# Remainder evictions of a six-layer cross network in pieces of 256 columns instead of 512

## The chip, the cores and the metric

The kernel runs on one core of a Trainium2 chip. The metric is the device time of one execution in microseconds (us), the median of several runs. A core has five engines that run their own queues of instructions and wait for one another by semaphores: TensorE (PE in the profile; its weight loads are PEld), VectorE (DVE), ScalarE (ACT), GpSimd (POOL) and SyncE (SP), which here issues most of the DMA transfers. Matrix products are summed in PSUM and leave it by an *eviction*: an instruction of ScalarE or VectorE that reads PSUM and writes SBUF.

## The reference

Six cross layers on 4096 rows of 416 columns, all in bf16:

```
B, F, D, L = 4096, 26, 16, 6        # Din = F * D = 416
x = x0
for l in range(6):
    x = x0 * (x @ ws[l] + bs[l]) + x
return x
```

ws[l] is 416 x 416, bs[l] has 416 entries.

## The kernel before

The kernel carries a sum c instead of x: with c the running sum of all (x @ ws + bs) plus one, the next x is x0 * c. The first five layers work on the transposed input, with features on the 128 partitions and rows of the batch along the free dimension; the last layer turns the product round, so that its results come out with batch rows on the partitions and can be stored.

416 features are three blocks of 128 (index m or k, NK = 3) and a remainder of 32. The batch of 4096 rows is two halves (s = 0, 1) of 2048, each of four groups (g) of 512 rows (CW). The main blocks of c and x are the tiles CM and XH. The remainder's 32 features would use a quarter of the partitions, so the four groups of a half are laid on partitions 32 g to 32 g + 31: the remainder of one half is a tile of 128 partitions by 512 columns, and both halves together are CR (c), XR (x).

In PSUM there is one pool of four buffers, each of two banks of 512 fp32 columns, which are given out in turn. A main tile (s, m) takes two buffers (h = 0, 1), the remainder sums of both halves take one (pr in layer 0, pr2 after it, one bank for each half).

Layer 0 (`first_layer`) works on XM0 as it arrives by DMA. In its second half (s = 1) the remainder sums of both halves are computed behind the main ones (`mm_rem`, lines 220 and 224) and evicted by `ew_rem`. Layers 1 to 4 take the six main tiles in pairs. TensorE multiplies the first tile's 48 matmuls (L208), then the rows that bring in the remainder of x for both tiles (L214, eight matmuls), then the second tile's 48. Behind the first pair of each layer stands `rem_pair`: the remainder sums of both halves, and their `ew_rem`.

A main eviction (`ew_main`, L187) is one ScalarE instruction over 1024 columns that adds the bias and writes a temporary tile t (a pool of six buffers); VectorE adds t to c (L188) and multiplies by x0 (L189), which gives the next x. `ew_rem` does the same for one half of the remainder with 512 columns: ScalarE L194 (layer 0, straight into CR) or L197 (into t), VectorE L198 (the addition, in layers 1 to 4) and L201 (the product with x0: in layer 0 two instructions of 256 columns, otherwise one of 512).

In layer 4 the finished c is sent back to batch rows by transposing DMAs from SP's queue: CM into XLrows, and CR into the scratch tiles scrR, whose rows ScalarE copies into XLrows by `xl_rem(s)` (L310). `xl_rem(0)` stands between two main evictions of layer 4, `xl_rem(1)` behind the last. The last layer (L359 to L380) sums into the tiles py; ScalarE casts them to bf16 (L405), VectorE adds XLrows (L407) and multiplies by the input rows (L395), and the result is stored (L396), the last piece by a DMA that ScalarE issues itself.

The order on each engine is the program's order where `pin` is used (`keep_in_program_order`); otherwise the tile framework may move an instruction.

Of the kernel before, what the change touches and what calls it, by code (L numbers as in the profile page):

```python
# [9 lines left out]
ACT = mybir.ActivationFunctionType  # L10
ALU = mybir.AluOpType
BF16 = mybir.dt.bfloat16
# [4 lines left out]
def kernel(  # L17
# [7 lines left out]
    nc = tc.nc  # L25
    B, D = x0.shape
    L = ws.shape[0]
    P = 128
    NK = 3
# [3 lines left out]
    NG = 4  # L33
    CW = 512
# [6 lines left out]
    tpool = ctx.enter_context(tc.tile_pool(name="tpool", bufs=6))  # L41
# [15 lines left out]
    bR = const.tile([P, L], FP32)  # L57
    X0rows = big.tile([P, NBT, D], BF16)
    XLrows = big.tile([P, NBT, D], BF16)
    scrR = [big.tile([P, 4, P], BF16, name=f"scrR{s}") for s in range(NS)]  # L60
# [5 lines left out]
    XR = [big.tile([P, NS * CW], BF16, name=f"XR{i}") for i in range(3)]  # L66
    CM = big.tile([P, NK, B], BF16, name="CM")
    CR = big.tile([P, NS * CW], BF16, name="CR")
# [11 lines left out]
    def pin(ins):  # L80
        tc.keep_in_program_order(ins)
# [33 lines left out]
    for g in range(1, NG):  # L115
        dst, src = WR[32 * g:32 * g + 32, 0, :], WR[0:R, 0, :]
# [73 lines left out]

    def ew_rem(l, s, pr, nxtR):
        cols = slice(CW * s, CW * s + CW)
        if l == 0:
            nc.scalar.activation(CR[:, cols], pr, ACT.Identity, bias=bR[:, 0:1], scale=1.0)  # L194
        else:
            tr = tpool.tile([P, 2 * CW], BF16, name="t")
            nc.scalar.activation(tr[:, 0:CW], pr, ACT.Identity, bias=bR[:, l:l + 1], scale=1.0)  # L197
            nc.vector.tensor_tensor(out=CR[:, cols], in0=tr[:, 0:CW], in1=CR[:, cols], op=ALU.add)  # L198
        for a in range(CW * s, CW * s + CW, CW if l else CW // 2):
            part = slice(a, a + (CW if l else CW // 2))  # L200
            prod = nc.vector.tensor_tensor(out=nxtR[:, part], in0=CR[:, part], in1=XR[0][:, part], op=ALU.mult)  # L201
            if l == 0:
                pin(prod)

    def mm_full(l, s, m, g, pts, cur, first, last):
        for k in range(NK):
# [27 lines left out]
    def first_layer(s):  # L234
# [53 lines left out]
        for m in range(2):  # L288
            ew_main(0, s, m, 1, pb[m], nxt)
        ew_rem(0, 0, pr[:, 0, :], nxtR)  # L290
        ew_main(0, s, 2, 1, pb[2], nxt)
        ew_rem(0, 1, pr[:, 1, :], nxtR)

    bias_setup()
# [4 lines left out]
    def rem_pair(l, cur, curR, nxtR, feeds_last):  # L299
        pr2 = psum.tile([P, 2, CW], FP32, tag="ps", name="pr2")  # L300
        for s in range(NS):
            mm_rem(l, s, pr2[:, s, :], cur, curR)
        for s in range(NS):
            ew_rem(l, s, pr2[:, s, :], nxtR)
            if feeds_last:
                nc.sync.dma_start_transpose(out=scrR[s][:], in_=CR[:, CW * s:CW * s + CW])

    def xl_rem(s):
        tc.keep_in_program_order(
            nc.scalar.copy(XLrows[:, 16 * s:16 * s + 16, NK * P:D].rearrange("p (g i) r -> p i g r", g=NG),  # L310
                           scrR[s][:].rearrange("p i (g r) -> p i g r", g=NG)))

    cur, curR = XH[0:2], XR[1]
    for l in range(1, LL):
        nxt, nxtR = [[h for h in XH if h is not cur[0] and h is not cur[1]][0], cur[0]], XR[1 + (l % 2)]
# [11 lines left out]
        for n in range(0, len(tiles), 2):  # L327
            ta, tb = tiles[n], tiles[n + 1]
            pts[ta] = new_pts()
            for g in range(NG):  # L330
                mm_full(l, ta[0], ta[1], g, pts[ta], cur, True, False)
            mm_row(l, ta[0], ta[1], pts[ta], curR, False, True)
            pts[tb] = new_pts()
            mm_row(l, tb[0], tb[1], pts[tb], curR, True, False)
            if feeds_last and n == 4:
                xl_rem(0)
            finish(ta)
            for g in range(NG):
                mm_full(l, tb[0], tb[1], g, pts[tb], cur, False, True)
            finish(tb)  # L340
            if n == 0:
                rem_pair(l, cur, curR, nxtR, feeds_last)
        if feeds_last:
            xl_rem(1)
        cur, curR = nxt, nxtR

    l = LL
# [123 lines left out]
```

## Time and profile before

| | |
|---|---|
| median of 3 runs (lowest, highest) | 130.42 us (130.15, 130.46) |
| the profiled execution | 130.23 us |
| its span, first to last instruction | 128.1 us |
| TensorE, VectorE, ScalarE, GpSimd busy | 123.5, 100.9, 86.2, 4.8 us |
| mean granted TensorE clock | 0.998 of full speed |
| ScalarE, 128 x 512 from PSUM, layers 1 to 4 (L197) | 8 times, 683 ns mean |
| ScalarE, 128 x 512 from PSUM, layer 0 (L194) | 2 times, 692 ns mean |
| ScalarE, copy 128 x 512 (L310) | 2 times, 626 ns mean |

A row of an engine's busy time counts each instruction from its start to its end; instructions that follow one another on ScalarE or VectorE overlap a little in the record. A row of instructions reads: line, engine, operation, output tile, input tiles, partitions and columns, how often, busy us, mean ns of one, and the idle time of the engine just before them with what ended it. A row of a timeline has the start in us, the length in us, the same names, and in brackets the idle time before it and its releaser.

### The profile page before, as it was taken

To read this page: it belongs to the slowest core of one execution; us is meant where nothing else is said; L and a number is where in the kernel's file an instruction comes from. 1 tells how busy PE (TensorE), PEld (TensorE's weight loads), DVE (VectorE), ACT (ScalarE), POOL (GpSimd) and SP (SyncE) were. 2 spreads that over 40 slices of the span, in tenths; PEclk is the share of its full clock that TensorE was granted. 3 is DMA by queue.
4 is the path that set the end of the run, shared out by engine and by line. 5 is a ranking of instruction groups with operands and counts; after the bars stand their busy time and mean duration, and the time that the engine had idled before them with its cause. 6 is when DMAs were issued, how large, how long until landed. Compare 5 with 4: busy or idle time off the path is not lost.

```text
span 128.1 us, 4002 instructions
## 1 busy us (share of the span) xinstructions
PE 123.5 (96%) x1708; PEld 55.9 (44%) x1710; DVE 100.9 (79%) x195; ACT 86.2 (67%) x98; POOL 4.8 (4%) x18
## 2 busy tenths in 40 slices
PE   7999999999999999999999999999999999999980
PEld 3343343444434444434444434444434445445450
DVE  0123579964979898989898989898989899988991
ACT  0048857878848668848668848668849696569660
POOL 4004001300000000000000000000000000000000
PEclk9999999999999999999999999999999999999999
DMA  3999999999940000000000000000498899976764
GB/s 93 234 234 224 174 238 259 318 332 336 336 144 0 5 0 0 8 0 5 0 5 0 5 0 5 0 0 5 86 125 192 161 135 236 199 231 220 228 194 142
DMA packets 42229, 16.37 MB, mean 128 GB/s; under 512 B 31034, under 2 KB 42212, under 8 KB 42212
## 3 DMA queue, kind: packets, MB, share of 16 engines
q1 hardware_dynamic: 37432, 15.40, 53.3%
q10 hardware_dynamic: 4780, 0.72, 3.6%
q8 instruction: 13, 0.21, 0.7%
q14 instruction: 4, 0.03, 0.1%
HBM read 6.15 MB, written 3.41 MB: 75 GB/s over the span
## 4 chain that ended last, share of the span: by engine, by line
PE 92%; DMA 4%; DVEq 1%; ACT 0%; issue 0%; DVE 0%
PE pt L208 50%; PE ph L240 13%; PE py L365 12%; PE pt L214 5%; PE pr L224 5%; DMA XM<-in_x_dram 4%; PE pr L220 2%; PE py L377 1%; PE ph L247 1%; PE py L380 1%; PE py L359 1%; DVEq L466 1%; PE tpr L163 1%; ACT t L405 0%; PE py L369 0%
## 5 line engine op out<-in xcount | busy, mean ns | idle before, releaser
L208 PE MATMUL pt<-XH,WM 128*32 128x512 bf16 x1152 | 65.2, 379 | 0.0
L187 ACT ACTIVATE t<-pt,bM 128x1024 bf16<-128x1024 f32 x48 | 49.6, 1115 | 19.3 <-PE pt L214 19.3
L208 PEld LDWEIGHTS <-WM 128*32 128x32 bf16 x1152 | 29.7, 97 | 33.8 <-issue 5.1
L188 DVE TENSOR_TENSOR CM<-t,CM 128x1024 bf16<-128x1024 bf16 x48 | 32.9, 686 | 5.1 <-ACT t L187 5.1
L189 DVE TENSOR_TENSOR XH<-CM,XM 128x1024 bf16<-128x1024 bf16 x48 | 33.2, 692 | 3.6
L405 ACT CAST t<-py 128x416 bf16<-128x416 f32 (+1 forms) x22 | 14.3, 649 | 5.1 <-PE py L365 2.0
L365 PE MATMUL py<-WM,XH 128*128 128x416 bf16 x90 | 17.0, 339 | 0.0
L240 PE MATMUL ph<-XM,WM 128*128 128x512 bf16 x70 | 16.3, 379 | 0.2
L181 ACT ACTIVATE CM<-ph,bM 128x1024 bf16<-128x1024 f32 x12 | 12.5, 1113 | 3.5 <-PE ph L247 3.5
L183 DVE TENSOR_TENSOR XH<-CM,XM 128x512 bf16<-128x512 bf16 x24 | 9.1, 438 | 3.6 <-ACT CM L181 3.6
L365 PEld LDWEIGHTS <-XH 128*128 128x128 bf16 x90 | 8.5, 98 | 7.6 <-issue 1.4
L240 PEld LDWEIGHTS <-WM 128*128 128x128 bf16 x72 | 6.8, 97 | 8.6 <-issue 1.1
L407 DVE TENSOR_TENSOR t<-t,XLrows 128x416 bf16<-128x416 bf16 (+1 forms) x20 | 9.3, 467 | 1.1 <-ACT t L405 1.1
L395 DVE TENSOR_TENSOR o<-t,X0rows 128x416 bf16<-128x416 bf16 (+1 forms) x22 | 9.9, 456 | 0.1
L214 PE MATMUL pt<-XR,WR 32*128 32x512 bf16 x96 | 7.3, 379 | 0.0
L224 PE MATMUL pr<-XH,WM 128*32 128x512 bf16 x96 | 6.6, 379 | 0.0
L197 ACT ACTIVATE t<-pr,bR 128x512 bf16<-128x512 f32 x8 | 5.1, 683 | 2.1 <-PE pr L224 2.1
L114 ACT ACT_TABLE_LOAD x1 | 1.3, 1283 | 6.1 <-DMA XM<-in_x_dram 6.1
L201 DVE TENSOR_TENSOR XR<-CR,XR 128x512 bf16<-128x512 bf16 (+1 forms) x12 | 4.4, 379 | 1.1 <-ACT CR L194 0.8
L224 PEld LDWEIGHTS <-WM 128*32 128x32 bf16 x120 | 3.2, 97 | 3.2
L148 PE MATMUL wps<-const-float32-1.0 128*128 128x512 f32 x4 | 3.8, 1094 | 0.8 <-PEq L455 0.8
L157 DVE CAST bM<-pb 128x18 f32<-128x18 bf16 x1 | 0.2, 177 | 4.9 <-PE pb L156 4.9
(52 smaller groups left out, 47.2 us busy)
## 6 DMA issues: line engine op xcount, KB each, us to landing
X0rows<-in_x_dram SPq DMA_DIRECT2D x8, 312.0 KB, 6.7
out_dram<-o SPq DMA_DIRECT2D x9, 208.0 KB, 3.2
WM<-in_ws_dram SPq DMA_DIRECT2D x5, 312.0 KB
out_dram<-o SPq DMA_DIRECT2D x13, 104.0 KB, 1.7
X0rows<-in_x_dram SPq DMA_DIRECT2D x4, 208.0 KB, 6.1
WR<-in_ws_dram SPq DMA_DIRECT2D x4, 130.0 KB, 4.8
WM<-in_ws_dram ACTq DMA_DIRECT2D x1, 312.0 KB
XM<-in_x_dram SPq DMA_TRANSPOSE x8, 5.7
```

Of the source, the lines that this page charges most:

```text
L181: nc.scalar.activation(c, src, ACT.Identity, bias=bias, scale=1.0)
L187: nc.scalar.activation(t[:], src, ACT.Identity, bias=bias, scale=1.0)
L188: nc.vector.tensor_tensor(out=c, in0=t[:], in1=c, op=ALU.add)
L189: nc.vector.tensor_tensor(out=x, in0=c, in1=XM0[:, m, c0:c0 + 2 * CW], op=ALU.mult)
L208: nc.tensor.matmul(pts[g // 2][32 * q:32 * q + 32, g % 2, :], lhsT=WM[:, l, k, 128 * m + 32 * q:128 * m + 32 * q + 32], rhs=cur[s][:, k, C ...
L214: nc.tensor.matmul(pts[g // 2][:, g % 2, :], lhsT=WR[32 * g:32 * g + 32, l, 128 * m:128 * m + 128], rhs=curR[32 * g:32 * g + 32, CW * s:CW ...
L224: nc.tensor.matmul(pr[32 * g:32 * g + 32, :], lhsT=WM[:, l, k, NK * P:D], rhs=cur[s][:, k, CW * g:CW * g + CW], start=False, stop=(k == NK ...
L240: nc.tensor.matmul(pt[:, gl, :], lhsT=WM[:, 0, k, 128 * m:128 * m + 128], rhs=cur[:, k, c0:c0 + CW], start=(k == 0 and not after_row), sto ...
L365: nc.tensor.matmul(py[:, 0:D], lhsT=q_x(q, g, k), rhs=WM[:, l, k, :], start=((not closes) and k == 0), stop=(closes and not adds and k == ...
L395: pin(nc.vector.tensor_tensor(out=o[:, 0:n, :], in0=src, in1=X0rows[:, b, :], op=ALU.mult))
L405: nc.scalar.copy(tv, src)
L407: pin(nc.vector.tensor_tensor(out=tv, in0=tv, in1=XLrows[:, rows(q, g0, n), :], op=ALU.add))
```

## The change

`ew_rem` evicts in two pieces of 256 columns. In layer 0 each of the two products of 256 columns can begin when its piece is there; in layers 1 to 4 the addition and the product stay whole. `xl_rem(0)` copies in two pieces (two of the four row blocks each), `xl_rem(1)` in one as before. ScalarE has 11 more instructions: two in layer 0, eight in layers 1 to 4, one for the copy.

```
     def ew_rem(l, s, pr, nxtR):
         cols = slice(CW * s, CW * s + CW)
+        halves = [slice(a, a + CW // 2) for a in range(0, CW, CW // 2)]
+        base = CR[:, cols] if l == 0 else tpool.tile([P, 2 * CW], BF16, name="t")
+        for a in halves:
+            nc.scalar.activation(base[:, a], pr[:, a], ACT.Identity, bias=bR[:, l:l + 1], scale=1.0)
         if l == 0:
-            nc.scalar.activation(CR[:, cols], pr, ACT.Identity, bias=bR[:, 0:1], scale=1.0)
-        else:
-            tr = tpool.tile([P, 2 * CW], BF16, name="t")
-            nc.scalar.activation(tr[:, 0:CW], pr, ACT.Identity, bias=bR[:, l:l + 1], scale=1.0)
-            nc.vector.tensor_tensor(out=CR[:, cols], in0=tr[:, 0:CW], in1=CR[:, cols], op=ALU.add)
-        for a in range(CW * s, CW * s + CW, CW if l else CW // 2):
-            part = slice(a, a + (CW if l else CW // 2))
-            prod = nc.vector.tensor_tensor(out=nxtR[:, part], in0=CR[:, part], in1=XR[0][:, part], op=ALU.mult)
-            if l == 0:
-                pin(prod)
+            for a in halves:
+                part = slice(CW * s + a.start, CW * s + a.stop)
+                pin(nc.vector.tensor_tensor(out=nxtR[:, part], in0=CR[:, part], in1=XR[0][:, part], op=ALU.mult))
+            return
+        nc.vector.tensor_tensor(out=CR[:, cols], in0=base[:, 0:CW], in1=CR[:, cols], op=ALU.add)
+        nc.vector.tensor_tensor(out=nxtR[:, cols], in0=CR[:, cols], in1=XR[0][:, cols], op=ALU.mult)
...
     def xl_rem(s):
-        tc.keep_in_program_order(
-            nc.scalar.copy(XLrows[:, 16 * s:16 * s + 16, NK * P:D].rearrange("p (g i) r -> p i g r", g=NG),
-                           scrR[s][:].rearrange("p i (g r) -> p i g r", g=NG)))
+        dst = XLrows[:, 16 * s:16 * s + 16, NK * P:D].rearrange("p (g i) r -> p i g r", g=NG)
+        src = scrR[s][:].rearrange("p i (g r) -> p i g r", g=NG)
+        n = 4 if s else 2
+        for i in range(0, 4, n):
+            pin(nc.scalar.copy(dst[:, i:i + n], src[:, i:i + n]))
```

## The prediction

> **What bounds the kernel now.** I read the page's busy rows and its chain first, then the list of what TensorE waits for, then the code-load queues, and last the timelines of ScalarE, VectorE and TensorE around each remainder eviction. The page:
>
> ```profile
> span 128.1 us, 4002 instructions
> PE 123.5 (96%) x1708; PEld 55.9 (44%) x1710; DVE 100.9 (79%) x195; ACT 86.2 (67%) x98; POOL 4.8 (4%) x18
> ...
> q8 instruction: 13, 0.21, 0.7%
> q14 instruction: 4, 0.03, 0.1%
> ...
> PE 92%; DMA 4%; DVEq 1%; ACT 0%; issue 0%; DVE 0%
> ...
> L187 ACT ACTIVATE t<-pt,bM 128x1024 bf16<-128x1024 f32 x48 | 49.6, 1115 | 19.3 <-PE pt L214 19.3
> ...
> L197 ACT ACTIVATE t<-pr,bR 128x512 bf16<-128x512 f32 x8 | 5.1, 683 | 2.1 <-PE pr L224 2.1
> ```
>
> TensorE is busy 96% of the span and makes 92% of the chain that ended last; ScalarE is 0% of it, is busy 67%, and sits idle 19.3 us before the main evictions, each time released by TensorE (L214). The rows of TensorE's own waits are short:
>
> ```profile
> engine line waited for: us in total, times, longest us
> PE wps L148 <- PEq L455: 0.8, 1, 0.8
> ```
>
> Its only wait is the one before its first instruction. So nothing that ScalarE or VectorE does today holds TensorE up, and the question is whether the change makes it do so. ScalarE's timeline (start, length, then in brackets the idle time before), for the remainder pair of layer 0, the pair of layer 1, and the copy of remainder rows:
>
> ```profile
> 26.66 1.27 ACT L194 ACTIVATE CR<-pr,bR 128x512 bf16<-128x512 f32 x2
> 29.41 4.13 ACT L187 ACTIVATE t<-pt,bM 128x1024 bf16<-128x1024 f32 x4 [1.48 <-PE pt L214]
> 34.07 1.27 ACT L197 ACTIVATE t<-pr,bR 128x512 bf16<-128x512 f32 x2 [0.54 <-PE pr L224]
> 36.97 4.13 ACT L187 ACTIVATE t<-pt,bM 128x1024 bf16<-128x1024 f32 x4 [1.64 <-PE pt L214]
> ...
> 98.81 0.62 ACT L310 COPY XLrows<-scrR 128x512 bf16<-128x512 bf16 x1
> 100.52 4.13 ACT L187 ACTIVATE t<-pt,bM 128x1024 bf16<-128x1024 f32 x4 [1.09 <-PE pt L214]
> ```
>
> Behind each lies idle time that TensorE ends: 1.48, 1.64 and 1.09 us. The pairs of layers 2 to 4 (53.31, 72.55, 91.78) have 1.63 or 1.64 us behind them in the same timeline. The consumers in layer 1, on VectorE:
>
> ```profile
> 35.88 0.42 DVE L198 TENSOR_TENSOR CR<-t,CR 128x512 bf16<-128x512 bf16 x1
> 36.33 0.42 DVE L201 TENSOR_TENSOR XR<-CR,XR 128x512 bf16<-128x512 bf16 x1
> 36.67 0.42 DVE L198 TENSOR_TENSOR CR<-t,CR 128x512 bf16<-128x512 bf16 x1
> ```
>
> Neither add waits for ScalarE (no bracket): VectorE comes late to them from its own queue. And on TensorE, the rows that write the bank next:
>
> ```profile
> 28.98 0.61 PE L214 MATMUL pt<-XR,WR 32*128 32x512 bf16 x8
> ...
> 36.54 0.61 PE L214 MATMUL pt<-XR,WR 32*128 32x512 bf16 x8
> ```
>
> **The change, part by part: the evictions.** Ten evictions of 512 columns (two in layer 0, eight in layers 1 to 4) become twenty of 256. No row before has a 256-column ScalarE eviction, so I work it out. Four 1024-column evictions back to back take 4.13 us and one lasts 1.115, so they start (4.13 - 1.115) / 3 = 1.005 us apart. Two of 512 take 1.27 and one lasts 0.683, so they start 0.59 apart. That is 0.415 us for 512 columns, 0.81 ns a column, and some 0.17 us that each instruction costs whatever its size. A half then starts 0.59 - 0.21 = 0.38 after the one before and lasts 0.683 - 0.21 = 0.47. Four halves: 3 x 0.38 + 0.47 = 1.61 us in place of 1.27, so +0.34 a pair. Bounds: nothing (no cost beside the columns), and a half that costs as much as a whole, 3 x 0.59 + 0.68 = 2.45, so +1.18. I take +0.34, from the straight line through two rows of the same operation; over five pairs it is 1.7 us of ScalarE time.
>
> The Trainium skill's page "ScalarE: Activation LUTs" (Rules for kernel authors) has about 0.3 us for each ACTIVATE and 0.83 ns an element, and "VectorE: DVE Perf Modes" (The TRN2 errata) advises tiles of 512 elements or more since a fixed cost is paid per instruction: both speak against halves. The rows bear out the slope and have 0.17 of fixed cost between starts, against 0.3; by the page's figure a pair would cost +0.6, an estimate, inside the bounds above, and the time would be the same.
>
> What hides it, place by place. (1) ScalarE's queue: behind the pair stands the L187 eviction of the next main tile, which TensorE releases at 36.97. The halves end at 34.07 + 1.61 = 35.68, at worst at 36.52. (2) The bank: PSUM's four buffers go round in order, so the remainder pair's buffer is the one that the second half of the second following tile takes, four allocations on. The last two of the eight L214 matmuls write it first: 36.54 + 6 x 0.067 (0.54 / 8 from the chain) = 36.94. Released at 35.68, it leaves 1.26 us; at worst 0.42. (3) VectorE: its add for the first 512 columns begins at 35.88 and needs two halves, ready at 34.07 + 0.38 + 0.47 = 34.92 (worst 35.34); the second begins at 36.67 and needs all four, 35.68 (worst 36.52). No new wait. Layers 2 to 4 have the same pattern, VectorE's adds a little later after the pair (55.32 after 53.31). In these layers the halves bring no overlap: the add reads all 512 columns and waits for both.
>
> Layer 0, whose pair starts at 26.66: halves ready at 27.13, 27.51, 27.89, 28.27, the worst case 27.35, 27.94, 28.53, 29.12. Here each 256-column product on VectorE now waits for its own half. The first may start before its 27.38 of today, where VectorE sat idle 0.82 us; the second, which started at once behind it, is ready from 27.51, and 0.5 us later in the worst case. Behind it in VectorE's queue stand two L183 products (27.79) and the second pair of halves (28.46). At worst this string ends at 29.12 + 0.29 = 29.4. VectorE next waits for ScalarE until 30.56 in any case, and TensorE reads the first 512 columns of XR at 28.98 (ready by 28.2 at worst) and the second at 32.98. The bank is written next at 28.98 + 6 x 0.067 = 29.38; the worst case frees it at 29.12. So layer 0 is hidden too, with 0.26 us left at the worst and 1.1 as I take it. The earlier start of the first product buys nothing: no one waits for it.
>
> **The copy.** One of 0.62 us becomes two: between 0.31 each (nothing added) and 0.62 each (+0.62); I take the fixed 0.17. ScalarE is idle 1.09 us behind it, and VectorE first reads these rows in the additions of the last layer, from 107.12 on, 7.7 us after the copy's end. Without that cover the next main eviction, and with it the buffers that the last layer's first sums take, would be late by the excess over 1.09. SP, POOL and their DMAs issue the same transfers in the same order; TensorE's instructions and VectorE's keep their order and number.
>
> **The sum.** The profiled execution took 130.23 us, 128.1 of it the span and 2.13 around it. Added to the path: 5 x 0.34 + 0.17, all in ScalarE's idle time, so 0. That gives 130.23; the median of the runs shown is 130.42, 0.19 above. I forecast 130.4.
>
> **The rivals.**
>
> (A) *TensorE waits for the remainder bank: slower.* It decides once four halves end after 36.94 in layer 1, that is 4s + 0.09 > 2.87, s > 0.69 us from one half's start to the next, more than the 0.59 of a whole. At s = 0.75 the stall is 4 x 0.75 + 0.09 - 2.87 = 0.22 us a layer, at four layers 0.9, and in layer 0, where the limit is 29.38 - 26.66 = 2.72, 0.37: 130.4 + 1.3 = 131.7. For it: no 256-column eviction has been seen here. Against it: fewer columns would have to cost more. Chance 0.05.
>
> (B) *A code load lands where the end waits for it: slower.* The program carries 11 more ScalarE instructions. The q14 row shows four loads; 0.1% of 16 engines' span over four is 0.001 x 16 x 128.1 / 4 = 0.51 us each (0.26 to 0.77 by the rounding). If ScalarE's next load falls in the last microseconds, where its cast and its output DMA are on the path, the end moves by such a load: 130.4 + 0.5 = 130.9. For it: ScalarE issues the last DMA. Against it: TensorE's 13 loads (q8, 0.007 x 16 x 128.1 / 13 = 1.1 us each) cost it no wait at all. Chance 0.14. "Runtime: NRT & Kernel Launch" (Instruction fetch mechanics) of the Trainium skill says that the next block is fetched while the current one runs and the crossing is mostly hidden; by that this rival is void, and TensorE's rows agree.
>
> (C) *The same load is now in the tail and moves out of it: faster.* Then the change saves up to one load, 130.4 - 0.5 = 129.9. For it: only lead-in and tail are not TensorE's (5.79 us to the first matmul with data, 128.1 - 124.4 = 3.7 after its last), so only there could time be found. Against it: no row of the tail shows an engine waiting for code. Chance 0.15.
>
> (D) *The split does nothing that overlaps.* In layers 1 to 4 this is so by the add over 512 columns; the time is the forecast's.
>
> **How the numbers follow.** The forecast with D 0.66, A 0.05, B 0.14, C 0.15. Runs of the kernel before lie between 130.15 and 130.46, so about 0.3% (0.39 us) is what can be told from no change: same 0.66, slower 0.05 + 0.14 = 0.19, faster 0.15. The range 129.9 to 131.0 holds the forecast with its scatter, B's 130.9 and C's 129.9 with half of their spread to either side, and leaves out A and the far halves of B and C, about 0.05 + 0.03 + 0.07 = 0.15. The worst case of the unknown costs adds nothing to the path, so it does not widen it.
>
> **What would show it.** Right: the list of TensorE's waits still has only the one at the start; the pair of L196 evictions takes about 1.6 us with some 1.3 idle after it; the 256-column row lasts about 470 ns; ScalarE's busy time grows by some 10 x (2 x 0.47 - 0.68) + 0.2 = 2.8 us to 89; the chain keeps TensorE at 92%. Wrong: a TensorE wait on ScalarE at L208 or L214; L202 released by ScalarE late in layers 1 to 4; a changed lead-in or tail with the same middle.

## The result, and the profile after

The changed kernel took 129.81 us (median of 9 runs, 129.75 to 130.14), the kernel before 130.19 (9 runs, 130.04 to 130.49): ratio 0.9968, 95% interval 0.9958 to 0.9978. It is 0.3% faster. The forecast of no change, and the range from 129.9, were wrong. Loaded anew, the changed kernel took 129.96, beside 130.23 for the kernel before.

Each run lists its time and its span. The difference, *the time outside the span*, is what settles this case:

| | time, median | span, median (range) | outside the span, median (range) |
|---|---|---|---|
| changed kernel, 9 runs | 129.81 | 128.0 (128.0 to 128.3) | 1.77 (1.75 to 1.84) |
| kernel before, 31 runs beside the first experiments | 130.23 | 128.1 (128.0 to 128.6) | 2.10 (2.06 to 2.16) |

0.33 us is gone outside the span, where no instruction of the kernel is recorded; the two ranges do not touch. The spans overlap. The profile after shows a middle that is as forecast. The page:

```profile
span 128.1 us, 4013 instructions
PE 123.6 (97%) x1708; PEld 55.8 (44%) x1710; DVE 100.8 (79%) x195; ACT 87.7 (68%) x109; POOL 5.4 (4%) x18
...
q14 instruction: 5, 0.04, 0.1%
...
PE 96%; DVEq 1%; ACT 0%; issue 0%; DVE 0%
...
L187 ACT ACTIVATE t<-pt,bM 128x1024 bf16<-128x1024 f32 x48 | 49.5, 1114 | 17.4 <-PE pt L214 17.4
...
L196 ACT ACTIVATE t<-pr,bR 128x256 bf16<-128x256 f32 x16 | 6.3, 474 | 2.1 <-PE pr L224 2.1
```

The span is that of before to a tenth. A half lasts 474 ns. The idle time before the main evictions fell from 19.3 to 17.4: ScalarE paid the halves from it. The chain reads 96% TensorE in place of 92% and 4% DMA only because the lead-in is now followed back through the filler matmuls. One row has a new number: five code loads (DMA transfers that bring an engine its next instructions) in q14, against four. TensorE's waits and ScalarE's timeline:

```profile
engine line waited for: us in total, times, longest us
PE wps L148 <- PEq L457: 0.8, 1, 0.8
```

```profile
26.62 1.57 ACT L196 ACTIVATE CR<-pr,bR 128x256 bf16<-128x256 f32 x4
...
34.03 1.56 ACT L196 ACTIVATE t<-pr,bR 128x256 bf16<-128x256 f32 x4 [0.54 <-PE pr L224]
36.93 4.13 ACT L187 ACTIVATE t<-pt,bM 128x1024 bf16<-128x1024 f32 x4 [1.33 <-PE pt L214]
...
99.13 0.71 ACT L313 COPY XLrows<-scrR 128x256 bf16<-128x256 bf16 x2 [0.36 <-DMA scrR<-CR]
100.48 4.13 ACT L187 ACTIVATE t<-pt,bM 128x1024 bf16<-128x1024 f32 x4 [0.64 <-PE pt L214]
```

TensorE still waits only for its start. Four halves take 1.56 us, and 1.33 us of idle time remain behind them. The copy pair takes 0.71, with 0.64 left even though it began 0.36 late behind its DMA. VectorE's add in layer 1 began at 35.84 and waited for nothing. And where is the fifth load? The DMA view of the stretch from 126 us to the end, when the last stores land, for the changed kernel:

```profile
## 3 DMA queue, kind: packets, MB, share of 16 engines
q1 hardware_dynamic: 145, 0.11, 16.6%
q10 hardware_dynamic: 144, 0.11, 14.7%
q14 instruction: 1, 0.01, 1.6%
```

In the kernel before, the same stretch has the rows of q1 and q10 and none of q14. A code load has come into the end of the span, as the rivals on code loads had it, and the time has fallen outside. Not all of q14's loads are ScalarE's: in experiments below, 11 more instructions on SP move the load at 122.55 us to 118.66, and 11 on VectorE move the one at 108.61 to 104.89. ScalarE's in the changed kernel are those at 52.78 and 126.89.

### The profile page after: what moved, and what is told of

It is laid out like the page before. It is cut to its first block, busy times and chain, and to the rows that moved or that the text cites. A ratio compares the mean times of both kernels' runs of the same rounds, so it can differ in the third digit from the quotient of the medians.

```text
span 128.1 us, 4013 instructions
## 1 busy us (share of the span) xinstructions
PE 123.6 (97%) x1708; PEld 55.8 (44%) x1710; DVE 100.8 (79%) x195; ACT 87.7 (68%) x109; POOL 5.4 (4%) x18
## 4 chain that ended last, share of the span: by engine, by line
PE 96%; DVEq 1%; ACT 0%; issue 0%; DVE 0%
PE pt L208 50%; PE ph L240 12%; PE py L367 12%; PE pt L214 5%; PE pr L224 5%; PE wps L148 4%; PE pr L220 2%; PE py L379 1%; PE ph L247 1%; PE py L382 1%; PE py L361 1%; DVEq L468 1%; ACT t L407 0%; PE py L371 0%; PE tpr L163 0%
## 5 line engine op out<-in xcount | busy, mean ns | idle before, releaser
L187 ACT ACTIVATE t<-pt,bM 128x1024 bf16<-128x1024 f32 x48 | 49.5, 1114 | 17.4 <-PE pt L214 17.4
L196 ACT ACTIVATE t<-pr,bR 128x256 bf16<-128x256 f32 x16 | 6.3, 474 | 2.1 <-PE pr L224 2.1
L220 PE MATMUL pr<-XR,WD 128*32 128x512 bf16 x40 | 3.9, 380 | 0.0
```

The source lines that it names most:

```text
L187: nc.scalar.activation(t[:], src, ACT.Identity, bias=bias, scale=1.0)
```

## The experiments

Theory 1: the number of ScalarE instructions decides, because it sets which instruction is the first of the next block of code; passing into it costs ScalarE a pause, which counts only if the others wait for ScalarE just then. Theory 2: the splits free something on the path. Each experiment was timed beside the kernel before on the same chip (31 to 35 runs of it a group); its time outside the span was 2.10 or 2.11 in all four groups.

### Instructions without splits, splits without all the instructions

Eleven and six added instructions (before each L187 after the remainder pair), evictions whole:

```
                 rem_pair(l, cur, curR, nxtR, feeds_last)
+                for _ in range([3, 3, 3, 2][l - 1]):      # [2, 2, 1, 1] for six
+                    pin(nc.scalar.activation(dz[:, 1:2], dz[:, 0:1], ACT.Identity, bias=dz[:, 0:1], scale=1.0))
```

> The kernel before, all evictions and copies whole, with 11 added ScalarE instructions that write one unused column (three behind the remainder pair of layers 1 to 3, two in layer 4). Theory 1 (count: the 11 instructions move a code load of ScalarE from behind the span into it): five loads in the q14 row, span 128.1 us, time 129.8, some 0.38 below the kernel before. Theory 2 (the split evictions free something that lies on the path): nothing is split, so the time is that of the kernel before, 130.2, ratio 1.000.

> As the run with 11 added instructions, but 6 (two, two, one, one). ScalarE's load near 54 us comes about 62 recorded instructions into its queue, the next would come 128 later at about 190; the kernel before records 183. Theory 1: 183 + 6 = 189 is at or just short of that, so four loads and 130.2 us, or, if the boundary lies one or two earlier, five loads and 129.8; in between nothing. Theory 2: 130.2.

Evictions split, copy whole (ten more instructions), and layer 0's evictions with the copy split (three more):

```
-        for i in range(0, 4, n):
-            pin(nc.scalar.copy(dst[:, i:i + n], src[:, i:i + n]))
+        tc.keep_in_program_order(nc.scalar.copy(dst, src))
```

> The changed kernel with the copy of remainder rows whole: ten more ScalarE instructions. Theory 1: 183 + 10 = 193 is past the boundary at about 190, so five loads and 129.8 us. Theory 2, if the evictions do it: 129.8 too; if the copy does it: 130.2.

```
         if l == 0:
-            nc.scalar.activation(CR[:, cols], pr, ACT.Identity, bias=bR[:, 0:1], scale=1.0)
+            for a in range(0, CW, CW // 2):
+                nc.scalar.activation(CR[:, CW * s + a:CW * s + a + CW // 2], pr[:, a:a + CW // 2], ...)
...
+        # copy as in the changed kernel
```

> Only layer 0's evictions and the one copy in halves: three more ScalarE instructions. Theory 1: 186 is short of 190, four loads, 130.2 us. Theory 2: these are the only places where a half lets something begin earlier, so the whole gain would show, 129.8.

| | time | ratio (95%) | span, median | outside, median |
|---|---|---|---|---|
| +11, nothing split | 129.97 | 0.9978 (0.9969 to 0.9987) | 128.2 | 1.79 |
| +6, nothing split | 130.07 | 0.9982 (0.9970 to 0.9995) | 128.3 | 1.79 |
| +10, all evictions split | 130.19 | 0.9996 (0.9986 to 1.0006) | 128.4 | 1.80 |
| +3, layer 0 and the copy split | 129.95 | 0.9979 (0.9969 to 0.9989) | 128.1 | 1.85 |

Theory 2 falls with the first row: the gain comes with nothing split. (Its q14 row counts six, not the five expected; one is a packet of 40 bytes at the start.) Theory 1 missed too: with three and six more, where the page's q14 row still has four loads, the gain was there; with ten it was not.

The page's row ends with the span, but the DMA view takes a window that reaches past it. There the traces hold a q14 load 0.6 us behind the end with ten more (128.96, span 128.4) and 1.3 us behind it with six (129.56, span 128.3), where the changed kernel has it at 126.89. With fewer instructions the load comes later, as a fixed place in the queue would have it. For the kernel before, and in this profile with three, none is recorded behind the span.

The run with ten shows why the gain was not there. Its span is 0.3 longer, and that lies in the program's last barriers. The instructions of the program's end (L466) from 127 us on, with lengths in ns and first and last start; first the kernel before, then the one with ten split evictions:

```profile
L466 ACTq EVENT_SEMAPHORE  x2: 17/17/17, 127.6 to 128.1; - x2
...
L466 ACTq DRAIN  x1: 8/8/8, 127.7 to 127.7; - x1
L466 DVEq DRAIN  x1: 19/19/19, 127.7 to 127.7; - x1
```

```profile
L466 ACTq EVENT_SEMAPHORE  x2: 17/17/17, 127.7 to 128.3; - x2
...
L466 DVEq DRAIN  x1: 19/19/19, 127.8 to 127.8; - x1
...
L466 ACTq DRAIN  x1: 136/136/136, 128.0 to 128.0; - x1
```

ScalarE leaves the first barrier (127.7), then its next instruction, a drain that takes 8 ns before, starts only at 128.0 and takes 136. VectorE's is done at 127.8. The second barrier, and the end, wait for ScalarE. I read this as the pause itself, some 0.3 us, seen inside the span. So I took theory 1 in a second form: the pause sits at a fixed place of ScalarE's code. Before, it would stand behind the span, where the end waits for it (2.10); no instruction recorded there shows it. Ten more instructions bring it onto the drain between the barriers (1.80 outside, 0.3 more inside). Eleven bring it onto the wait before, which lasts for the stores anyway.

### One block of code further, and other queues

Drains that do nothing were put on one engine's queue behind each pair of main tiles (117, 10 or 24 on ScalarE, 11 on GpSimd), the 117 into the changed kernel, the others into the kernel before:

```
             finish(tb)
+            for _ in range([10, 10, 10, 10, 10, 10, 10, 10, 10, 9, 9, 9][3 * (l - 1) + n // 2]):
+                pin(nc.scalar.drain())
```

> The changed kernel, everything split as in it, with 117 empty ScalarE instructions (drains, some ten behind each pair of main tiles in layers 1 to 4): 11 + 117 = 128 more than before, one 8 KB block of 64-byte instructions. Theory 1, now: where ScalarE's queue passes from one block of 128 instructions to the next it stands still for some 0.35 us; in the kernel before this falls behind the span, where the end waits for it (2.10 us outside the span), and 11 more instructions bring it into the wait for the last stores (1.78). With 128 more the passage is back where it was: 2.10 outside the span, 130.2 us, ratio 1.000. Theory 2 (the splits themselves bring the gain): 1.78 outside and 129.8.

> The kernel before with ten drains on ScalarE's queue, nothing split. Theory 1: as with ten split evictions, the passage falls on the drain between the two barriers at the end: that drain starts some 0.35 us late, the span is 128.4 instead of 128.1, 1.79 outside it, time 130.2. Theory 2: 130.2 with 128.1 and 2.10.

> The kernel before with 24 drains on ScalarE's queue, nothing split. Theory 1: the passage falls 13 instructions earlier than in the changed kernel, among the last casts; ScalarE's queue runs ahead of the engine there, so it may hide: span 128.1, outside 1.78, time 129.9; if it doesn't hide, a cast starts 0.35 late and the span is up to 128.4. Theory 2: 130.2.

> The kernel before with 11 drains on GpSimd's queue in place of ScalarE's. Theory 1: GpSimd's 35 instructions stay inside one block of 128, so nothing moves: 2.10 outside, 130.2. A third theory, that any program with other code is placed better: 1.78 outside, 129.9.

| | time | ratio (95%) | span, median | outside, median |
|---|---|---|---|---|
| changed kernel +117 (128 more than before) | 130.38 | 1.0004 (0.9996 to 1.0013) | 128.3 | 2.11 |
| +10 drains | 130.18 | 0.9993 (0.9984 to 1.0001) | 128.4 | 1.81 |
| +24 drains | 129.96 | 0.9980 (0.9970 to 0.9990) | 128.15 | 1.80 |
| +11 drains on GpSimd | 130.27 | 0.9999 (0.9989 to 1.0009) | 128.2 | 2.10 |

All four came out as the second form has it. The first row is the change undone without touching it: every eviction and the copy in halves, and 117 empty instructions take the whole gain away. With ten drains, the late second drain is there again without a split, its line in the same view, taken from 125 us on and so with the first drain (158 ns) as well:

```profile
L468 ACTq DRAIN  x2: 135/146/158, 125.8 to 128.0; - x2
```

and 24 hide the pause in the last stage. Other code on another engine does nothing. The place returns after 128 instructions, and a q14 load is 0.04 MB / 5 = 8 KB. The traces agree: with the 117 drains ScalarE's loads stand at 42.42 and 83.92 us, behind 67 and 191 of its recorded instructions, and none follows; in the changed kernel they stand behind 63 and 191.

### Near the edge, and other engines

> The kernel before with three drains on ScalarE's queue, nothing split; against the kernel with layer 0 and the copy split, which has three more instructions as well and 1.85 us outside the span. Theory 1: 1.85 outside here too, span 128.1 to 128.2, time 130.0. If the split of layer 0 had a part in it: 2.10 outside and 130.3.

> The kernel before with one drain on ScalarE's queue. Theory 1: the passage moves by one instruction of the program's end. If the exposed stretch outside the span is longer than one instruction, 2.10 stays and 130.3; if the kernel before stood at its edge, 1.85 and 130.0. Both fit the theory; the run shows how far the kernel before was from the gain.

> The changed kernel with 11 drains on SP's queue in layers 1 to 4. If SP passes a block in the part that the end waits for, the 1.78 outside falls further, towards 1.4, and the time to 129.5; if it passes one elsewhere, nothing moves: 1.78 and 129.85. If the 11 bring a passage of SP's into the tail, up to 0.35 more.

> The same with 11 drains on VectorE's queue. Same readings: below 1.78 outside if VectorE's passage was exposed, 1.78 if not, up to 0.35 more in the span or outside if it becomes so. A drain in VectorE's queue costs it less than the 0.3 us that it waits at each pair of tiles, so layers 1 to 4 keep their length.

The same edit with [1, 1, 1, 0, ...] and [1, 0, ...] on ScalarE in the kernel before, and 11 drains on SP's or VectorE's queue in the changed kernel.

| | time | ratio (95%) | outside, median (range) |
|---|---|---|---|
| +3 drains | 130.49 | 1.0007 (0.9995 to 1.0019) | 2.27 (1.83 to 2.47) |
| +1 drain | 130.15 | 0.9990 (0.9979 to 1.0000) | 1.89 (1.88 to 1.98) |
| changed, +11 on SP | 130.01 | 0.9975 (0.9963 to 0.9987) | 1.81 (1.74 to 1.86) |
| changed, +11 on VectorE | 129.92 | 0.9973 (0.9963 to 0.9983) | 1.81 (1.75 to 1.83) |

One instruction is enough for most of the gain outside the span (1.89 against 2.11), though the interval of its time still reaches 1.0000. SP and VectorE bring nothing more, and no version beats the changed kernel. Three drains did not fit: 5 of 12 runs at 1.83 to 1.86, 7 at 2.23 to 2.47. So that kernel, the changed one and the three splits were loaded anew, with three added activations on dz ([1, 1, 1, 0]) beside them:

> The same kernel as the run with three drains, loaded anew. If the 1.83 to 2.47 us outside the span belong to this code, they come again, with some runs at 1.83 and most above 2.2; if they were this one load of the program, all runs lie at 1.85 and the time at 130.0.

> Three added ScalarE instructions that write an unused column, in place of three drains. The count alone decides: the same distribution as with three drains. What the added instructions are, or where they stand, decides: 1.85 as with three split ones.

> Layer 0 and the copy split, loaded anew. Count and code decide: 1.85 outside again, 130.0. Each load of a program decides: some other value between 1.8 and 2.5.

> The changed kernel, loaded anew. 1.77 outside as in its nine runs, span 128.0 to 128.3, ratio 0.997. If each load decides, another value.

| | time | ratio (95%) | outside, median (range) | runs of 12 above 2.1 |
|---|---|---|---|---|
| +3 drains again | 130.06 | 0.9998 (0.9984 to 1.0013) | 1.88 (1.82 to 2.44) | 4 |
| +3 added activations | 129.95 | 0.9976 (0.9967 to 0.9985) | 1.82 (1.80 to 1.90) | 0 |
| +3 splits again | 130.02 | 0.9982 (0.9970 to 0.9995) | 1.84 (1.80 to 2.40) | 2 |
| changed kernel again | 129.96 | 0.9979 (0.9967 to 0.9991) | 1.79 (1.75 to 1.86) | 0 |

With three more instructions the end has two outcomes, some 1.85 and 2.2 to 2.5, and the share of the second differs between kernels and loads (7, 4, 0, 0 and 2 runs). It is neither the load alone nor the kind of instruction alone. The five kept profiles add one thing: the two with the long end (2.47 and 2.36 outside) hold a q14 load behind the span, at 130.24 and 130.39 us, and the three with the short end (1.80 to 1.86) hold none. What tips it was not found. The changed kernel's 1.77 is stable (1.79 loaded anew, 1.86 at the most).

## Why the prediction was wrong

The step that failed is the last line of the sum. It set the profiled run's 130.23 us against "128.1 of it the span and 2.13 around it", added nothing to the path, "so 0. That gives 130.23", and so took the 2.13 as given. It is not given: 0.33 of it goes (2.10 to 1.77) when ScalarE has 11 more instructions, split or not, and comes back when it has 128 more. The account that fits is ScalarE's pause at the next block of code, which the 11 instructions move into the wait for the last stores; the pause was seen with ten more, not in the kernel before, where it would stand behind the span. A smaller part of the miss has another source: the sum gave 130.23, and the forecast took 130.4 from a median of three runs, where nine runs gave 130.19.

Rival C named the mechanism and gave it 0.15, with the cost as one load (0.51 us by the q14 row). The weight against it was the sentence "no row of the tail shows an engine waiting for code". That is true of the span and says nothing of the time behind it, which no row of the page covers. The prediction had the difference between time and span, 2.13, and did not ask what fills it. The size was off as well: the pause costs 0.33 outside the span, or 0.3 as seen at the late drain, not a load's 0.51. And the q14 row was read as ScalarE's alone; of its four loads inside the span only the one at 54.39 us moves with ScalarE's instructions (to 51.42 with 24 more).

Rival B was the same pause brought into the span, and it exists: ten instructions do it (128.4). The time stays that of the kernel before all the same (130.19 against 130.23), since the pause no longer counts behind the span. With eleven it does not lengthen the span, one instruction apart. The weight that TensorE's 13 loads without a wait had against B was misplaced: those loads pass in the middle of the kernel, and the pause that counts stands at its end. The Trainium skill, "Runtime: NRT & Kernel Launch" (Instruction fetch mechanics), says that code comes in blocks of 16 KiB and that the crossing is mostly hidden. Here TensorE's loads have that size (0.21 MB / 13) and hide. ScalarE's are 8 KB and return after 128 instructions, and at the end the crossing costs 0.3 us. The measurement decides.

The rest held. The halves: four in 1.56 us forecast at 1.61, a half 474 ns forecast at 470, idle time behind them 1.33 forecast at 1.3, no wait on TensorE, so rival A is void. ScalarE's busy time grew by 1.5 us, not 2.8: I added record lengths, which overlap, where the row counts their union, 5 x 0.3. Rival D is right, and so is what the prediction said of layer 0: the earlier start there is worth nothing either. Theory 2's best case, layer 0 and the copy alone, gains no more (129.95, 130.02) than three activations that do nothing (129.95).

Of the first ratio, 0.9968, a part is scatter of the span, which ran from 128.0 to 128.6 in the 31 runs of the kernel before. Loaded anew, the changed kernel gave 0.9979. Outside the span the two agree, 1.77 and 1.79.

## What to carry to other kernels

Where time and span are both listed, subtract them before calling a change free: a different number of instructions on one engine can move the time at the program's end, by the account above because that engine's code block boundary moves in or out of it; here that was worth 0.33 us or 0.25%. The DMA view with a window past the span's end can help: it showed the load there with ten and with six more, though not in the kernel before. A gain or a loss of a few tenths from an edit that the path does not see should first be tried with as many instructions that do nothing, and with one block more (128 on ScalarE) to undo it. A kernel tuned to such a place keeps the gain only while the count stays clear of it: eleven and 24 more had it, ten and 128 more did not.

## What the runs showed of the hardware that was not expected

- The pause at a block of code: the drain between the last barriers started 0.3 us late and took 136 ns in place of 8, with ten more instructions on ScalarE, whether these were split evictions or drains.
- The loads of q14, which ScalarE, VectorE and SP share, are 8 KB (0.04 MB over five), and the effect returns after 128 ScalarE instructions (2.10 outside, then 2.11); TensorE's are 16 KB (0.21 MB over 13).
- Fewer instructions on ScalarE bring the q14 load that I take for its last later: 121.31 us with 24 more, 126.89 in the changed kernel, 128.96 with ten split evictions, 129.56 with six, and 130.24 or 130.39 in the long ends with three.
- Three instructions past the kernel before, the end has two outcomes 0.4 to 0.6 us apart in runs of one program (1.83 to 1.86 and 2.23 to 2.47). The long ends that were profiled hold a code load behind the span, the short ones none. The cause is open.
- Why a pause one, three or six instructions earlier than in the kernel before, still behind the span, costs less there (1.79 to 1.89 outside with one, six and, mostly, three more) is open too: no instructions are recorded behind the span, only DMA transfers.
